# Linear attention and two MLPs in one program: the second product of the first MLP done two token blocks at a time, 512 columns a matmul

## The chip, the core and the metric

The kernel runs on one core of one Trainium2 chip. The metric is the device time of that core for one execution, in microseconds (us). TensorE (PE) multiplies, VectorE (DVE) and ScalarE (ACT) work element by element, GpSimd (POOL) does next to nothing here, and SyncE (SP) issues nearly all transfers (DMA) between device memory and the on-chip buffers.

## The reference

```python
kv  = einsum('bhsd,bhse->bhde', k, v)         # 8 batches, 8 heads, 576 steps, 64 wide
out = einsum('bhsd,bhde->bhse', q, kv)
x   = out / sqrt(mean(out*out) + 1e-6) * g_norm     # -> 4608 tokens x 512
h   = x @ moe_w_in                            # 512 -> 2048
x   = maximum(0.01*h, h) @ moe_w_out          # 2048 -> 512
h   = maximum(x @ moe2_w_in, 0)               # 512 -> 2048
out = (h*h) @ moe2_w_out                      # 2048 -> 512
```

All data is float32.

## The kernel before

The 4608 tokens are nine blocks (0 to 8) of 512. The program has four passes, each over all blocks: pass 1 is the attention and the first product with its leaky ReLU, pass 2 the second product of the first MLP, passes 3 and 4 the two products of the second MLP.

Every float32 operand is split into a high part (rounded to the format that TensorE reads at full rate, an ACT copy) and a low part (the rest, a DVE subtraction); a product is three matmuls: high by high, high by low, low by high. Passes 2 to 4 save further multiplications by a Strassen scheme in Winograd's form: both operands are cut into quarters (A11 to A22 for the weights, B11 to B22 for the activations in pass 2), sums of quarters are made (S1 to S4 from A, T1 to T4 from B), and seven products P1 to P7 of half size replace eight. `PRODUCTS` names their operands, `ORDER` the order in which they run, `SUMS` the sums. The weight sides of all seven are made in pass 1 and kept in device memory.

Pass 2 before goes block by block. A block's contraction of 2048 is cut in four groups n (`NQ`), and for each group `load_g2` loads two halves of the activations (`g_raw`), `sum_op` makes the four T sums on DVE, `hi_op` and `lo_op` make the seven operand pairs, and `second` issues 12 matmuls for each of the seven products: two chunks c, two output halves t, three split products. B's quarters split the block's 512 tokens in two halves of 256 (`U`), so every matmul of this pass moves 256 columns. The seven products add up in seven banks of the accumulation memory (PSUM) over the four groups. At a block's last group the banks are read and combined (`p1`, `u2`, `u3`, `u4` and the four outputs C11 to C22, by the `adder` on DVE or an ACT copy), and stored to `x2_d`.

Pass 3 (`first`) takes block 0 alone with 256 columns a matmul, then blocks 1 to 8 in pairs, where B's two column halves are the two blocks of a pair (`SETS`), with 512 columns. It is the same operand form as pass 2 has after the change: weights stationary, activations moving.

The order of all this is a table: each step gets a time in slots (`at_slot`), the steps are sorted by it and issued in that order, so it fixes the order of every engine's queue. `tick` counts the slots and issues the stores that have waited one, and `fetch` loads weights. On-chip data lives in `NBIG` = 46 buffers of 4 KB a partition, handed out in the order in which they came free; 28 of them hold the weights of pass 2 all through that pass.

Of the kernel before, what the change touches and what calls it, by code (L numbers as in the profile page):

```python
# [10 lines left out]
F32 = mybir.dt.float32  # L11
# [7 lines left out]
def tile_linear_attention_two_mlps(  # L19
# [26 lines left out]
    nc = tc.nc  # L46
# [106 lines left out]
    def give_big(*ns):  # L153
        big_free.extend(ns)
# [108 lines left out]
    def store(out, in_, *slots):  # L263
        stores.append([out, in_, slots, 0])
# [22 lines left out]
        w_s[w, n, name] = t  # L287

    w_staged = {}
    w_names = [[PRODUCTS[p][x] for p in ORDER] for x in range(2)]  # L290

    def store_w2(w, n, x):
        name = w_names[LEFT[w]][x]
        slot, half = divmod(NPR * n + x, 2)
        src = w_operand(w, n, name)
        if (w, slot) not in w_staged:
            w_staged[w, slot] = take_big([P, 2, 2, 2, P], F32R, f"wh{name}_{w[0]}{w[1]}_{n}")
        t, s = w_staged[w, slot]
        nc.scalar.activation(out=t[:, half, 0], in_=src, func=AF.Copy)
        nc.vector.tensor_tensor(  # L300
            out=t[:, half, 1], in0=src, in1=f32(t[:, half, 0]), op=ALU.subtract
        )
        if half:
            store(w3_d[w][slot], f32(t).rearrange("p b h c f -> p b (h c f)"), s)
        if x == NPR - 1:
            give_big(w_s.pop((w, n))[1])


    def w_pos(w, n, x):
        name = w_names[LEFT[w]][x]  # L310
        if name[0] in "ST":
            y = int(name[1]) - 1
        else:
            i, j = int(name[1]) - 1, int(name[2]) - 1
            k, o = (j, i) if LEFT[w] == 0 else (i, j)
            y = 4 + 2 * (1 - k) + o
        return NPR * (n % 2) + y

    def store_a(w, n):
        to = w2_d[w][n // 2]  # L320
        if w[1] == 0:
            for name in ("A11", "A12", "A22"):
                at0 = w_pos(w, n, w_names[0].index(name))
# [518 lines left out]
    def second(ph, gg, x, free):  # L842
        j, n = gg
        tick()
        pr = ORDER[x]
        if n == 0:
            bank[pr] = next_bank(f"ps{ph}_{j}_{pr}")
        ps = bank[pr]
        gname = PRODUCTS[pr][1 - ph]
        g = op_t[ph, gg, gname][0]  # L850
        last = n == NQ - 1
        for c in range(2):
            w = w2((ph, 1), 2 * n + c, x)
# [12 lines left out]
        drop_op(ph, gg, gname)
        if not last:
            return
        if pr == 1:
# [3 lines left out]
            u_t["u2"] = adder("gl", f"u2_{ph}{j}", bank[6], p1)  # L873
        elif pr == 7:
            u_t["u3"] = adder("stg", f"u3_{ph}{j}", ps, u_t["u2"])
        elif pr == 5:
            u_t["u4"] = adder("gh", f"u4_{ph}{j}", ps, u_t["u2"])
        outs = {2: ("C11", "p1"), 5: ("C22", "u3"), 4: ("C21", "u3"), 3: ("C12", "u4")}
        if pr in outs:
            name, x = outs[pr]  # L880
            e = adder("h", f"o{ph}{j}_{name}", ps, u_t[x])
            i, o = int(name[1]) - 1, int(name[2]) - 1
            if ph == 0:
                to = x2_d[j][2 * i:2 * i + 2].rearrange("c p t -> p c t")[:, :, o * U:(o + 1) * U]
# [33 lines left out]
    with tc.manual_schedule():  # L918
# [71 lines left out]
        def at_slot(t, *st):  # L990
            ev.append((t, st))

        def prep(z):
            n = (("os", 1), ("os", 2), ("oh", 2), ("oh", 11), ("ol", 2), ("oh", 0), ("ol", 11),
                 ("os", 3), ("ol", 0), ("oh", 3), ("oh", 1), ("ol", 3), ("ol", 1), ("os", 4))
            if z == "S":
# [4 lines left out]
            assert n[3] == ("oh", 11)  # L1001
            return [(kind, names.get(x) or f"{z}{x}") for kind, x in n]

        def second_pass(t0, ph, blocks):
            gs = [(j, n) for j in blocks for n in range(NQ)]
            steps = prep("TS"[ph])
            for x, gg in enumerate(gs):
                at0 = t0 + NPR * x
                ahead = 13 if ph and not x else 8
                at_slot(at0 - 18 if ahead > 8 else max(at0 - 14, t0 - 12), "gl", ph, gg)  # L1010
                for n, (kind, name) in enumerate(steps):
                    at_slot(
                        at0 - ahead + n * (ahead - 1) / len(steps) + 0.3, kind, ph, gg, name
                    )
# [101 lines left out]
        def drop_pairs(ps):  # L1116
# [84 lines left out]
```

## Time and profile before

| what | us |
|---|---|
| median of 3 runs (lowest, highest) | 1590.11 (1588.51, 1590.2) |
| the profiled execution | 1588.2 |
| its span, first to last instruction | 1586.4 |
| TensorE busy within the span | 1570.8 |
| VectorE busy | 1199.6 |
| ScalarE busy | 804.2 |

The span is what the trace covers; the profiled execution's own time is 1.8 us longer. Busy times count instructions at work, not waiting. Matmuls are pipelined, so one matmul's duration in the trace is longer than the distance from its start to the next one's start; rates are read from starts. Pass 1 lies from 0 to 504.6 us of the span, pass 2 to 867.5, pass 3 to about 1222.8 and pass 4 to the end.

### The profile page before, as it was taken

The numbers are of one execution on the slowest core, as the hardware profiler recorded it, in microseconds if no ns is written. First come the engines' busy times: TensorE is split into PE (matmuls) and PEld (weight loads), VectorE is DVE, ScalarE is ACT, GpSimd is POOL, SyncE is SP. The second block draws the span as 40 slices with busy tenths as digits, with TensorE's granted clock in tenths as the row PEclk, the third lists the DMA queues.
The fourth block names the chain that finished last, engine by engine and source line by source line (L and its number), as shares of the span: only waits on it lengthen the run. The fifth ranks groups of instructions, "written<-read, shape, count | busy, mean of one in ns | idle before, by whom it ended". The sixth has DMA issues, their size and how long they took to land. (4 is left out here: it accounts for less than half of the span.)

```text
span 1586.4 us, 27414 instructions
## 1 busy us (share of the span) xinstructions
PE 1570.8 (99%) x10604; PEld 1425.4 (90%) x10604; DVE 1199.6 (76%) x1952; ACT 804.2 (51%) x1429; POOL 7.2 (0%) x16
## 2 busy tenths in 40 slices
PE   8999999999999999999999999999999999999998
PEld 5788888888888999999999888888888999999998
DVE  6857777777765888777777877768777887777775
ACT  6856666666655444444444444535446544433442
POOL 0000000000000000000000000000000000000000
PEclk9999999999999999999999999999999999999999
DMA  9978899899579344433349444555569443333341
GB/s 255 284 220 284 257 308 294 292 282 348 190 244 296 107 141 145 128 129 127 124 128 335 140 163 162 185 169 186 165 214 356 161 142 128 124 129 127 126 126 72
DMA packets 239714, 309.04 MB, mean 195 GB/s; under 512 B 52192, under 2 KB 190944, under 8 KB 239584
## 3 DMA queue, kind: packets, MB, share of 16 engines
q1 hardware_dynamic: 238224, 306.74, 59.7%
q8 instruction: 83, 1.36, 0.4%
q10 hardware_dynamic: 1360, 0.56, 0.1%
q14 instruction: 47, 0.39, 0.1%
HBM read 183.50 MB, written 123.73 MB: 194 GB/s over the span
## 5 line engine op out<-in xcount | busy, mean ns | idle before, releaser
L666 PE MATMUL hps<-xh,w 128*128 128x512 f32 x1152 | 378.7, 396 | 2.1 <-ACT xh L623 1.3
L666 PEld LDWEIGHTS hps<-xh,w 128*128 128x128 f32 x1152 | 216.1, 188 | 49.8 <-DVE w L238 1.9
L666 PE MATMUL hps<-xl,w 128*128 128x512 f32 x576 | 224.6, 390 | 0.5 <-DVE xl L624 0.5
L666 PEld LDWEIGHTS hps<-xl,w 128*128 128x128 f32 x576 | 108.4, 188 | 22.6 <-issue 1.0
L678 ACT ACTIVATE h<-hps 128x512 f32<-128x512 f32 x144 | 84.9, 592 | 25.0 <-issue 10.2
L775 DVE TENSOR_TENSOR h_C<-aps,u 128x512 f32<-128x512 f32 x72 | 49.5, 688 | 35.4 <-PE aps L796 35.1
L775 DVE TENSOR_TENSOR u<-bps,p 128x512 f32<-128x512 f32 x72 | 49.5, 687 | 28.6 <-ACT p L806 19.0
L380 DVE TENSOR_TENSOR w<-w 128x512 fp32r<-128x512 f32 x56 | 37.8, 687 | 34.8 <-ACT w L379 30.6
L553 DVE TENSOR_TENSOR qhl<-qtps,qhl 128x512 fp32r<-128x512 f32 x32 | 22.1, 691 | 46.2 <-ACT qhl L552 46.2
L806 ACT ACTIVATE p<-aps 128x512 f32<-128x512 f32 x36 | 21.3, 592 | 69.9 <-PE aps L796 69.9
L796 PE MATMUL aps<-op_B21h,w 128*128 128x512 f32 (+1 forms) x160 | 52.0, 374 | 1.2 <-ACT p L806 1.2
L796 PE MATMUL bps<-op_T4h,w 128*128 128x512 f32 (+1 forms) x160 | 51.2, 369 | 0.6 <-DVE u L775 0.6
L205 DVE SCALAR_TENSOR_TENSOR w_raw<-w_raw 128x512 uint32<-128x512 uint32 x64 | 44.1, 688 | 9.8 <-ACT w_raw L204 9.3
L796 PE MATMUL aps<-op_B22h,w 128*128 128x512 f32 (+1 forms) x160 | 51.1, 368 | 0.0
L796 PE MATMUL bps<-op_T3h,w 128*128 128x512 f32 (+1 forms) x160 | 51.0, 368 | 0.0
L796 PE MATMUL bps<-op_T2h,w 128*128 128x512 f32 (+1 forms) x160 | 51.0, 368 | 0.0
L796 PE MATMUL aps<-op_B11h,w 128*128 128x512 f32 (+1 forms) x160 | 51.0, 368 | 0.0
L796 PE MATMUL aps<-op_T1h,w 128*128 128x512 f32 (+1 forms) x160 | 51.0, 368 | 0.0
L813 ACT ACTIVATE h_C<-aps 128x512 f32<-128x512 f32 x36 | 21.5, 599 | 57.5 <-issue 38.1
L775 DVE TENSOR_TENSOR u<-ps,p 128x512 f32<-128x512 f32 x18 | 12.4, 692 | 49.6 <-ACT p L871 49.6
L611 DVE TENSOR_TENSOR sqo<-sqo,y 128x512 f32<-128x512 f32 x32 | 22.1, 692 | 35.3 <-ACT y L609 35.3
L552 ACT ACTIVATE qhl<-qtps 128x512 fp32r<-128x512 f32 x32 | 19.1, 597 | 52.3 <-PE qtps L545 52.3
(1430 smaller groups left out, 4096.4 us busy)
## 6 DMA issues: line engine op xcount, KB each, us to landing
g_raw<-g SPq DMA_DIRECT2D x144, 512.0 KB, 5.4
g<-h SPq DMA_DIRECT2D x144, 256.0 KB, 5.0
g<-h_C SPq DMA_DIRECT2D x144, 256.0 KB, 2.5
w_raw<-in_moe_w_in_dram SPq DMA_DIRECT2D x32, 512.0 KB, 6.8
w_raw<-in_moe_w_out_dram SPq DMA_DIRECT2D x32, 512.0 KB, 7.0
x_raw<-x SPq DMA_DIRECT2D x32, 512.0 KB, 6.5
w<-w SPq DMA_DIRECT2D x56, 256.0 KB, 4.7
w<-w SPq DMA_DIRECT2D x28, 512.0 KB, 5.4
```

Of the source, the lines that this page charges most:

```text
L205: nc.vector.scalar_tensor_tensor(out=lower, in0=upper, scalar=0x80000000, in1=lower, op0=ALU.bitwise_and, op1=ALU.bitwise_or,)
L380: nc.vector.tensor_tensor(out=by_h[:, :, 1], in0=src[:, :, 1], in1=src[:, :, 0], op=ALU.subtract)
L552: nc.scalar.activation(out=t[:, 0], in_=ps, func=AF.Copy)
L553: nc.vector.tensor_tensor(out=t[:, 1], in0=ps, in1=f32(t[:, 0]), op=ALU.subtract)
L611: (nc.gpsimd if i == 1 else nc.vector).tensor_tensor(out=osb, in0=osb, in1=y, op=ALU.mult)
L666: nc.tensor.matmul(out=ps, lhsT=w[:, wh, c * P:(c + 1) * P], rhs=x_t[j][xh, c // 2][0][:, c % 2, :], start=(c == 0 and y == 0), stop=(c == ...
L678: nc.scalar.activation(out=h, in_=h_ps.pop((j, m)), func=AF.Prelu, alpha=0.01)
L775: nc.vector.tensor_tensor(out=t, in0=x, in1=y, op=ALU.add)
L796: nc.tensor.matmul(out=ps[:, p], lhsT=w[:, wh, c, :], rhs=t[xh][:, c, :], start=(fresh and p == 0 and c == 0 and y == 0), stop=(p == len(p ...
L806: nc.scalar.activation(out=p1, in_=ps, func=AF.Copy)
L813: nc.scalar.activation(out=h, in_=ps, func=AF.Relu)
```

## The change

Blocks 1 to 8 of pass 2 are taken in four pairs, as pass 3 takes them: the two column halves of B are the two blocks, so a matmul moves 512 columns. Within a pair the work goes product by product, each over all four groups n, in the new order `ORDER2` = 1, 6, 7, 2, 5, 4, 3. P2 is added onto P1's banks and P3 onto P5's, after P1 and P5 have been read. The T sums are made in place, over the quarter that is no longer wanted, in another but equivalent form (`D_SUMS`), and B22 is loaded a second time for T1 and P3. Pass 1 stores its result for these blocks in two tiles a group (`h_d`), so that each load is one contiguous tile of 128 x 1024. Block 0 keeps the old form with the new order. What comes below is the new core; line offsets and the smaller renamings are left out.

```diff
+    ORDER2 = (1, 6, 7, 2, 5, 4, 3)
 ...
 def leaky(j, m):
-        store(
-            g_d[0][j][m // 4][:, m % 2, :, (m // 2 % 2) * U:(m // 2 % 2 + 1) * U],
-            h.rearrange("p (t u) -> p t u", t=2),
-        )
+        if j:
+            store(h_d[j][m % 2][m // 4][:, m // 2 % 2], h)
 ...
+    PLACE = {"T3": "B12", "T2": "B11", "T4": "T3", "T1": "T2"}
+    D_SUMS = {
+        "T3": ("B22", "B12", ALU.subtract), "T2": ("T3", "B11", ALU.add),
+        "T4": ("B21", "T2", ALU.subtract), "T1": ("B22", "T2", ALU.subtract),
+    }
+    def pair_load(z, name, n):
+        t, slot = take_big([P, 2, TB], F32, f"d{name}_{z}_{n}")
+        k, o = int(name[1]) - 1, int(name[2]) - 1
+        nc.sync.dma_start(out=t, in_=h_d[SETS[z][o]][k][n])
+    def pair_sum(z, name, n):
+        x, y, op = D_SUMS[name]
+        to = d_t[z, PLACE[name], n]
+        nc.vector.tensor_tensor(out=to[0], in0=d_t[z, x, n][0], in1=d_t[z, y, n][0], op=op)
+    def pair_hi(z, x, n):
+        ts, slots = zip(*(take_big([P, 2, TB], F32R, f"dop{z}_{name}_{n}" + "hl"[y]) for y in range(2)))
+        nc.scalar.activation(out=ts[0], in_=d_t[z, name, n][0], func=AF.Copy)
+    def pair_lo(z, x, n):
+        nc.vector.tensor_tensor(out=lo, in0=d_t[z, name, n][0], in1=f32(hi), op=ALU.subtract)
+    def pair_second(z, x, n):
+        at = {2: 1, 3: 5}.get(pr, pr)
+        if n == 0 and at == pr:
+            bank["d", pr] = [next_bank(f"dps{z}_{pr}_{t}", 1)[:, 0] for t in range(2)]
+        ps = bank["d", at]
+        for c in range(2):
+            w = w2((0, 1), 2 * n + c, x)
+            for t in range(2):
+                for y, (wh, gh) in enumerate(((0, 0), (0, 1), (1, 0))):
+                    nc.tensor.matmul(out=ps[t], lhsT=w[:, wh, t, :], rhs=ops[gh][:, c, :], ...)
+        ...
+            if pr == 1:
+                nc.scalar.activation(out=u_t["p1", t], in_=ps[t], func=AF.Copy)
+            elif pr == 6:
+                u_t["u2", t] = adder("du2", f"du2_{z}{t}", ps[t], u_t["p1", t])
+            elif pr == 7:
+                u_t["u3", t] = adder("du3", f"du3_{z}{t}", ps[t], u_t["u2", t])
 ...
+        def pairs_pass(t0):
+            for z in range(1, len(SETS)):
+                def at_unit(w, *st):
+                    at_slot(t0 + 2 * w - 5.4, *st)
+                for n in range(NQ):
+                    loads = ((-10.4, "B12"), (-6.8, "B22"), (-2.8, "B11"), (2.2, "B21"), (12.2, "B22"))
+                    sums = ((-4, "T3"), (0, "T2"), (8, "T4"), (15, "T1"))
 ...
-        t2 = second_pass(t1, 0, list(range(NB)))
+        t2 = pairs_pass(second_pass(t1, 0, [0]))
```

On PE, at the point where pass 2 goes from block 0 to block 1, this stood before: six matmuls of 256 columns by one weight tile, then the next weight tile, and another product after 12 (`ps0_1_6` is the bank of block 1, product 6; `w2_01` is a weight tile).

```order
L860 MATMUL ps0_0_3_5534<-op0_(0, 3)_B22_5765,w2_01_27_5405 128x256 x6
L860 MATMUL ps0_1_6_5927<-op0_(1, 0)_T2_5789,w2_01_0_3783 128x256 x6
L860 MATMUL ps0_1_6_5927<-op0_(1, 0)_T2_5789,w2_01_3_4772 128x256 x6
L860 MATMUL ps0_1_1_5944<-op0_(1, 0)_B11_5803,w2_01_0_3783 128x256 x6
L860 MATMUL ps0_1_1_5944<-op0_(1, 0)_B11_5803,w2_01_4_5034 128x256 x6
```

Now, at the same point on PE, pair 1 starts with product 1; `dps1_1_0` and `dps1_1_1` are its two banks, `dop1_B11_0h` and `_0l` the high and low operand of group 0.

```order
L872 MATMUL ps0_0_3_5566<-op0_(0, 3)_B22_5814,w2_01_27_5437 128x256 x6
L953 MATMUL dps1_1_0_5957<-dop1_B11_0h_5862,w2_01_0_3815 128x512
L953 MATMUL dps1_1_0_5957<-dop1_B11_0l_5863,w2_01_0_3815 128x512
...
L953 MATMUL dps1_1_1_5958<-dop1_B11_0h_5862,w2_01_0_3815 128x512
L953 MATMUL dps1_1_1_5958<-dop1_B11_0l_5863,w2_01_0_3815 128x512
...
L953 MATMUL dps1_1_0_5957<-dop1_B11_0h_5862,w2_01_3_4804 128x512
L953 MATMUL dps1_1_0_5957<-dop1_B11_0l_5863,w2_01_3_4804 128x512
```

The 12 matmuls of a product and group are now one unit of 12 x 512 columns, and the next unit is the same product's next group.

On DVE the queue of a group before (block 2, group 2) has four sums (`sT1` to `sT4`) between seven low parts, all 512 elements long.

```order
L737 TENSOR_TENSOR sT1_0_(2, 2)_6537<-g_raw0_2_2_0_6415 128x512
L737 TENSOR_TENSOR sT2_0_(2, 2)_6539<-g_raw0_2_2_1_6417,sT1_0_(2, 2)_6537 128x512
L757 TENSOR_TENSOR op0_(2, 2)_T2_6545<-sT2_0_(2, 2)_6539,op0_(2, 2)_T2_6545 128x512
L757 TENSOR_TENSOR op0_(2, 2)_B11_6559<-g_raw0_2_2_0_6415,op0_(2, 2)_B11_6559 128x512
L737 TENSOR_TENSOR sT3_0_(2, 2)_6577<-g_raw0_2_2_1_6417,g_raw0_2_2_0_6415 128x512
L757 TENSOR_TENSOR op0_(2, 2)_B21_6574<-g_raw0_2_2_1_6417,op0_(2, 2)_B21_6574 128x512
```

Now the densest stretch of DVE's queue in a pair, around the end of product 6 of pair 1: low parts of T3 (`dop1_T3_..l`), the T4 sums written over T3 (`dB12_1_..`), and the two `du2` additions that read product 6's banks.

```order
L936 TENSOR_TENSOR dop1_T3_1l_6083<-dB12_1_1_5685,dop1_T3_1h_6082 128x1024
L921 TENSOR_TENSOR dB12_1_1_5685<-dB21_1_1_5976,dB11_1_1_5829 128x1024
L787 TENSOR_TENSOR du2_10_6099<-dps1_6_0_6035,dp1_10_6027 128x512
L787 TENSOR_TENSOR du2_11_6101<-dps1_6_1_6036,dp1_11_6029 128x512
L936 TENSOR_TENSOR dop1_T3_2l_6104<-dB12_1_2_5721,dop1_T3_2h_6103 128x1024
L921 TENSOR_TENSOR dB12_1_2_5721<-dB21_1_2_5995,dB11_1_2_5860 128x1024
L936 TENSOR_TENSOR dop1_T3_3l_6123<-dB12_1_3_5758,dop1_T3_3h_6122 128x1024
```

Sums and low parts have twice the length and half the number, and a sum for a later product stands between the low parts of the present one.

## Rows read from the trace of the kernel before

**Rows 1.** Page: span, PE's busy time, granted clock by slice (9: full)
```profile
span 1586.4 us, 27414 instructions
PE 1570.8 (99%) x10604; PEld 1425.4 (90%) x10604; DVE 1199.6 (76%) x1952; ACT 804.2 (51%) x1429; POOL 7.2 (0%) x16
PEclk9999999999999999999999999999999999999999
```

**Rows 2.** PE's waits: who for whom, us in total, times, longest
```profile
PE ssps L592 <- ACT sqo L576: 1.9, 3, 1.3
...
PE aps L796 <- ACT p L806: 1.2, 3, 0.7
```

**Rows 3.** Stretches: us, busy by engine (instructions), clock, DMA share, GB/s
```profile
0.00:504.60 504.60, 496.84 (x2877) 407.52 (x2878) 346.43 (x660) 323.56 (x618) 7.20 (x16) 1.00 0.86 272
...
544.90:867.50 322.60, 322.60 (x2691) 322.60 (x2690) 260.93 (x416) 132.22 (x233) 0.00 (x0) 1.00 0.48 157
867.50:1222.80 355.30, 352.31 (x1723) 296.68 (x1722) 273.97 (x373) 177.24 (x276) 0.00 (x0) 1.00 0.58 192
```

**Rows 4.** PE's timeline: first matmul of block 1, of pass 3 (start, length)
```profile
544.90 0.88 PE L860 MATMUL ps<-op_(1, 0)_T,w 128*128 128x256 f32 x6
...
867.46 0.28 PE L796 MATMUL bps<-op_T2h,w 128*128 128x256 f32 x1
```

**Rows 5.** Chain of waits, pass 3 with 512 columns (start, length, matmuls)
```profile
1109.23 2.72 PE aps L796 x12
1111.95 1.36 PE bps L796 x6
```

**Rows 6.** Matmuls and weight loads of block 1, group 0: shortest, median, longest ns
```profile
L860 PEld LDWEIGHTS ps<-op_(1, 0)_T,w x48: 192/192/192, 544.8 to 553.3; 128*128 128x128 f32 x48
L860 PE MATMUL ps<-op_(1, 0)_T,w x48: 283/283/283, 544.9 to 553.4; 128*128 128x256 f32 x48
```

**Rows 7.** Groups of DVE and ACT in pass 3, by shape: busy us, mean ns
```profile
L775 DVE TENSOR_TENSOR u<-bps,p 128x512 f32<-128x512 f32 x68 | 46.7, 687 | 26.3 <-ACT p L806 16.7 <-PE bps L796 9.6
L737 DVE TENSOR_TENSOR sT<-x_raw,sT 128x1024 f32<-128x1024 f32 x13 | 15.9, 1221 | 0.2
L757 DVE TENSOR_TENSOR op_T2l<-sT,op_T2h 128x1024 fp32r<-128x1024 f32 x7 | 8.6, 1226 | 4.3 <-ACT op_T2h L752 4.3
L806 ACT ACTIVATE p<-aps 128x512 f32<-128x512 f32 x34 | 20.1, 591 | 67.0 <-PE aps L796 67.0
L752 ACT ACTIVATE op_T4h<-sT 128x1024 fp32r<-128x1024 f32 x7 | 7.4, 1062 | 13.3 <-DVE sT L737 13.3
```

**Rows 8.** Transfers issued from 545 to 867 us: count, KB, us to landing
```profile
g_raw<-g SPq DMA_DIRECT2D x60, 512.0 KB, 5.4
x<-o_C SPq DMA_DIRECT2D x35, 256.0 KB, 4.9
...
x_raw<-x SPq DMA_DIRECT2D x6, 512.0 KB, 7.3
```

**Rows 9.** Timeline of DVE, ACT and PE at the start of pass 3
```profile
866.83 0.68 DVE L757 TENSOR_TENSOR op_T1l<-sT,op_T1h 128x512 fp32r<-128x512 f32 x1
867.42 0.68 DVE L737 TENSOR_TENSOR sT<-x_raw,sT 128x512 f32<-128x512 f32 x1
868.03 0.68 DVE L775 TENSOR_TENSOR o_C<-ps,u 128x512 f32<-128x512 f32 x1
868.22 0.63 ACT L752 ACTIVATE op_T4h<-sT 128x512 fp32r<-128x512 f32 x1 [6.13 <-DVE sT L737]
868.76 0.62 ACT L752 ACTIVATE op_B22h<-x_raw 128x512 fp32r<-128x512 f32 x1
870.53 0.60 ACT L806 ACTIVATE p<-aps 128x512 f32<-128x512 f32 x1 [1.16 <-PE aps L796]
871.18 0.38 PE L796 MATMUL aps<-op_B21h,w 128*128 128x256 f32 x1 [0.69 <-ACT p L806]
```

More of the change, by code (lines that the diff above doesn't have):

```diff
@@ L132, in tile_linear_attention_two_mlps @@
     g_d = [
-        [[dram.tile([P, 2, 2, TB], F32, name=f"g{ph}_{j}_{n}") for n in range(NQ)] for j in range(NB)]
+        [[dram.tile([P, 2, 2, TB], F32, name=f"g{ph}_{j}_{n}") for n in range(NQ)]
+         for j in range(NB if ph else 1)]
         for ph in range(2)
     ]
+    h_d = {
+        j: [[dram.tile([P, 2, TB], F32, name=f"h{k}_{j}_{n}") for n in range(NQ)] for k in range(2)]
+        for j in range(1, NB)
+    }
     big_free = list(range(NBIG))
@@ L289, in tile_linear_attention_two_mlps @@
     w_staged = {}
-    w_names = [[PRODUCTS[p][x] for p in ORDER] for x in range(2)]
+    w_names = {
+        w: [PRODUCTS[p][LEFT[w]] for p in (ORDER if w[0] else ORDER2)] for w in LEFT
+    }
     def store_w2(w, n, x):
-        name = w_names[LEFT[w]][x]
+        name = w_names[w][x]
         slot, half = divmod(NPR * n + x, 2)
@@ L309, in w_pos @@
     def w_pos(w, n, x):
-        name = w_names[LEFT[w]][x]
+        name = w_names[w][x]
         if name[0] in "ST":
@@ L678, in leaky @@
         nc.scalar.activation(out=h, in_=h_ps.pop((j, m)), func=AF.Prelu, alpha=0.01)
-        store(
-            g_d[0][j][m // 4][:, m % 2, :, (m // 2 % 2) * U:(m // 2 % 2 + 1) * U],
-            h.rearrange("p (t u) -> p t u", t=2),
-        )
+        if j:
+            store(h_d[j][m % 2][m // 4][:, m // 2 % 2], h)
+        else:
+            store(
+                g_d[0][j][m // 4][:, m % 2, :, (m // 2 % 2) * U:(m // 2 % 2 + 1) * U],
+                h.rearrange("p (t u) -> p t u", t=2),
+            )
         tick()
@@ L844, in second @@
         tick()
-        pr = ORDER[x]
+        pr = (ORDER if ph else ORDER2)[x]
         if n == 0:
@@ L872, in second @@
             u_t["p1"] = p1
-            u_t["u2"] = adder("gl", f"u2_{ph}{j}", bank[6], p1)
+        if pr == (1 if ph else 6):
+            u_t["u2"] = adder("gl", f"u2_{ph}{j}", bank[6], u_t["p1"])
         elif pr == 7:
@@ new lines, in pair_sum @@
+    def pair_sum(z, name, n):
+        x, y, op = D_SUMS[name]
+        to = d_t[z, PLACE[name], n]
+        nc.vector.tensor_tensor(out=to[0], in0=d_t[z, x, n][0], in1=d_t[z, y, n][0], op=op)
+        del d_t[z, PLACE[name], n]
+        d_t[z, name, n] = to
+        if name == "T3":
+            give_big(d_t.pop((z, "B22", n))[1])
+    def pair_hi(z, x, n):
+        name = PRODUCTS[ORDER2[x]][1]
+        ts, slots = zip(*(take_big([P, 2, TB], F32R, f"dop{z}_{name}_{n}" + "hl"[y]) for y in range(2)))
+        nc.scalar.activation(out=ts[0], in_=d_t[z, name, n][0], func=AF.Copy)
+        d_op[z, x, n] = ts, slots
@@ new lines, in pair_lo @@
+    def pair_lo(z, x, n):
+        name = PRODUCTS[ORDER2[x]][1]
+        hi, lo = d_op[z, x, n][0]
+        nc.vector.tensor_tensor(out=lo, in0=d_t[z, name, n][0], in1=f32(hi), op=ALU.subtract)
+        if name in ("B21", "T1", "T4", "B22"):
+            give_big(d_t.pop((z, name, n))[1])
+    def pair_second(z, x, n):
+        tick()
+        pr = ORDER2[x]
+        at = {2: 1, 3: 5}.get(pr, pr)
+        if n == 0 and at == pr:
+            bank["d", pr] = [next_bank(f"dps{z}_{pr}_{t}", 1)[:, 0] for t in range(2)]
+        ps = bank["d", at]
+        ops, slots = d_op.pop((z, x, n))
+        last = n == NQ - 1
+        for c in range(2):
+            w = w2((0, 1), 2 * n + c, x)
+            for t in range(2):
+                for y, (wh, gh) in enumerate(((0, 0), (0, 1), (1, 0))):
+                    nc.tensor.matmul(
+                        out=ps[t], lhsT=w[:, wh, t, :], rhs=ops[gh][:, c, :],
+                        start=(n == 0 and at == pr and c == 0 and y == 0),
+                        stop=(last and c == 1 and y == 2),
+                        skip_group_check=True,
+                    )
+        give_big(*slots)
+        if z == len(SETS) - 1:
+            d_done.update(NPR * (2 * n + c) + x for c in range(2))
+            for slot in range(NSLOT):
+                if ((0, 1), slot) in w_t and {2 * slot, 2 * slot + 1} <= d_done:
+                    drop_w(((0, 1), slot))
+        if not last:
+            return
+        for t in range(2):
+            if pr == 1:
+                u_t["p1", t] = take_mid("dp", [P, TB], f"dp1_{z}{t}")
+                nc.scalar.activation(out=u_t["p1", t], in_=ps[t], func=AF.Copy)
[3 more added lines that the diff above has]
+                u_t["u3", t] = adder("du3", f"du3_{z}{t}", ps[t], u_t["u2", t])
+            else:
+                name = {2: "C11", 5: "C22", 4: "C21", 3: "C12"}[pr]
+                if pr == 2:
+                    e = hp.tile([P, TB], F32, tag="h", name=f"do{z}_{name}{t}")
+                    nc.scalar.activation(out=e, in_=ps[t], func=AF.Copy)
+                else:
+                    e = adder("h", f"do{z}_{name}{t}", ps[t], u_t["u2" if pr == 3 else "u3", t])
+                i, o = int(name[1]) - 1, int(name[2]) - 1
+                store(x2_d[SETS[z][o]][2 * i + t], e)
@@ L991, in at_slot, with prep @@
             ev.append((t, st))
-        def prep(z):
+        def prep(z, first=False):
             n = (("os", 1), ("os", 2), ("oh", 2), ("oh", 11), ("ol", 2), ("oh", 0), ("ol", 11),
                  ("os", 3), ("ol", 0), ("oh", 3), ("oh", 1), ("ol", 3), ("ol", 1), ("os", 4))
-            if z == "S":
+            if first:
+                n = (("os", 1), ("oh", 11), ("ol", 11), ("os", 2), ("oh", 2), ("ol", 2), ("os", 3),
+                     ("oh", 3), ("oh", 0), ("ol", 3), ("oh", 1), ("ol", 0), ("ol", 1), ("os", 4),
+                     ("oh", 4), ("ol", 4), ("oh", 22), ("ol", 22))
+            elif z == "S":
                 n += (("oh", 22), ("oh", 4), ("ol", 22), ("ol", 4))
@@ L1005, in second_pass @@
             gs = [(j, n) for j in blocks for n in range(NQ)]
-            steps = prep("TS"[ph])
+            steps = prep("TS"[ph], not ph)
             for x, gg in enumerate(gs):
@@ L1017, in second_pass @@
                     at_slot(at0 + n + 0.1, "s2", ph, gg, n, True)
-                if gg[0] == blocks[-1]:
+                if ph and gg[0] == blocks[-1]:
                     at_slot(at0 + NPR, "wd", (ph, 1), gg[1])
@@ L1022, in tile_linear_attention_two_mlps @@
         at_slot(0, "lag", 5)
+        def pairs_pass(t0):
[5 more added lines that the diff above has]
+                    sums = ((-4, "T3"), (0, "T2"), (8, "T4"), (15, "T1"))
+                    if z == 1:
+                        loads = ((-6.2, "B12"), (-6.1, "B22"), (-2.2, "B11"), *loads[3:])
+                        sums = ((-3, "T3"), *sums[1:])
+                    for w, name in loads:
+                        at_unit(w + n, "pl", z, name, n)
+                    for w, name in sums:
+                        at_unit(w + n + 0.02, "pt", z, name, n)
+                    for x in range(NPR):
+                        at_unit(NQ * x + n, "ph", z, x, n)
+                        at_unit(NQ * x + n + 0.01, "po", z, x, n)
+                        at_slot(t0 + 2 * (NQ * x + n) + 0.1, "p2", z, x, n)
+                t0 += 2 * NPR * NQ
+            return t0
         t1 = 0
-        t2 = second_pass(t1, 0, list(range(NB)))
+        t2 = pairs_pass(second_pass(t1, 0, [0]))
         last = len(SETS) - 1
```

12 lines of the change are left out of this document (9 added, 3 removed).

## The prediction

> **What bounds the kernel now.** I read the page first: TensorE is busy for 1570.8 of the span's 1586.4 us, and its granted clock stands at full (the 2.4 GHz level) in all 40 slices [rows 1]. Then the list of PE's waits: the longest is 1.9 us in total, the one at pass 3's start 1.2 us in three times [rows 2]. Then the stretches: in blocks 1 to 8 of pass 2, from 544.90 to 867.50, PE is busy for 322.60 of 322.60 us, while DVE is busy for 260.93, ACT for 132.22, and the transfers take 0.48 of their engines at 157 GB/s [rows 3]. So the stretch that the change rewrites is nothing but a row of matmuls, without a gap; time can only go by making these matmuls take less of PE, and come back only as gaps.
>
> What a matmul takes of PE is the distance between starts. Block 1 starts at 544.90 and pass 3 at 867.46 [rows 4]; between them lie 8 blocks x 4 groups x 7 products x 12 = 2688 matmuls of 256 columns, so one takes 322.56 / 2688 = 120.0 ns. In pass 3, 12 matmuls of 512 columns take 2.72 us, 226.7 ns each [rows 5]. Twice 256 columns cost 240.0 ns as two matmuls and 226.7 as one: 13.3 ns are a price of the matmul, not of its columns.
>
> **The change, part by part.** *Fewer and wider matmuls.* The pairs do 4 x 7 x 4 x 12 = 1344 matmuls of 512 columns in place of the 2688: 1344 x 226.7 ns = 304.7 us against 322.6. That is 17.9 us less. The same instruction (weights stationary, 512 columns moving, three split products a weight pair) runs in pass 3 at this rate while DVE and ACT work on operands of the same form, so I take the rate as it is. The clock needs no term, since PE stays without gaps on both sides.
>
> *Supplying a unit.* A unit is the 12 matmuls of one product and group, 2.72 us. It needs a high part (ACT, 1024 elements, 1.06 us) and a low part (DVE, 1.23 us) [rows 7]. Per pair DVE has 28 low parts and 16 sums at 1.22 us and 10 additions at 0.69: 53.7 + 6.9 = 60.6 us of 28 x 2.72 = 76.2, a share of 0.80, against 260.93 / 322.60 = 0.81 before [rows 3, 7]. ACT has 28 x 1.06 + 4 x 0.6 = 32 us. Neither becomes the bound on average.
>
> What could still hurt is the order within a pair. In the built order the high part of most units waits for the matmuls of the unit three before it, whose buffers it takes; from that release there are two units, 5.44 us, until PE wants it. In the densest place, the end of product 6 in the order shown, DVE has two additions (1.4), then the low part, whose high part ACT makes meanwhile, then a sum (1.22) that the next low part stands behind. Release, high part 1.06, low part 1.23 is 2.3 us; with a sum and the two additions wholly in the way, 2.3 + 1.22 + 1.38 = 4.9. Both are under 5.44, so I cost the supply at 0. Without this cover each us beyond 5.44 costs a third of a us per unit, since a buffer comes round every third unit.
>
> *Loads.* A pair loads five tiles of 512 KB for each group instead of four: 20 x 0.524 + 8 outputs x 0.262 = 12.6 MB in 76.2 us, 165 GB/s, near the 157 that this stretch moves now and below the 192 of pass 3 [rows 3]. A 512 KB load of pass 2 lands after 5.4 us, the slowest kind there after 7.3 [rows 8]. Each load stands in SP's queue 2.8 units or more (7.6 us; in pair 1 at least 2.2, 6.0 us) ahead of the sum or copy that reads it. The tightest is the second B22: its buffer is free only after B21's low part, and T1's sum, behind which DVE's queue waits, comes next. 7.6 us and the two units of lead behind it cover 7.3. Cost 0; at a landing of 12 us, which no row shows, it would cost about the 2 us of rival 2 a pair.
>
> *Pass 1.* The same 256 KB stores, each now one run a partition in place of two. PE's gaps of pass 1 (504.60 - 496.84 = 7.8 us [rows 3]) are at the start and wait for engines, not for these stores: 0. Block 0 in the order 1, 6, 7 starts with a plain quarter, so its first operand needs no sum ahead: 0.
>
> *PSUM.* A pair opens ten banks; product 4 takes those of P1 and P2, whose last reader, an ACT copy of 0.6 us, has all of product 5 (10.9 us) to finish. P2 is added to P1 after products 6 and 7. No wait.
>
> *Pair 4 to pass 3.* Here a wait grows. Before, PE stands 0.69 us for the copy `p`, which ends at 871.13 [rows 9]. Ahead of it on ACT are two high parts that hang on DVE's T4 sum. Before, one output addition of DVE lay behind that sum. Now the last product ends with two additions, the second released by PE's very last matmul, and both stand ahead of T1's low part and the sum. From PE's end: 0.1 for the release, two steps of 0.6 and the sum's 0.68 on DVE, then 0.54 (the two copies' distance) and 0.62 on ACT; so `p` can start at 3.2 us, where PE would let it start at 2.9 (24 matmuls x 0.12). The wait becomes about 1.0 us: +0.3 us (0, if DVE gains on this, to +0.9, if another addition falls in between).
>
> *Passes 3 and 4* keep their instructions and, as the built order shows, their leads; the buffers only come round in another order: 0.
>
> Sum against the profiled execution: 1588.2 - 17.9 + 0.3 = 1570.6 us. The three timed runs lie at 1588.51 to 1590.2 with the median at 1590.11; their mean is 1.4 us above the profiled one. I carry that: **1572.0 us**. For the likeliest case alone I would say 1569.5 to 1575.
>
> **A rule that speaks against this.** The 13.3 ns come from [rows 4, 5]. The Trainium skill (TensorE: Matmul & The Clock Gate, section "Back-to-back issue gap") gives the isolated gap of a matmul as its columns at 2.4 GHz plus about 2.5 ns. By that rule the change would save only 1344 x 2.5 ns = 3.4 us, an estimate that would put the time at 1586.5, on rival 1's side. The trace does not agree: 120.0 and 226.7 ns lie 13.3 and 13.4 above their columns at 2.4 GHz [rows 4, 5].
>
> **The rivals.**
>
> 1. *The width is not what costs.* In pass 2 each weight load lasts 192 ns beside a matmul distance of 120 [rows 6]; perhaps something in this pass, as the loading of its weights, sets the pace by the column, and 512 columns stay at 2 x 120.0 = 240 ns. Then the change does not do what it says, and the time is 1588.2 + 0.3 + 1.4 = 1589.9, no change. Against it: pass 3 also loads 128 x 128 weights for every matmul, and keeps 226.7 at 512 columns. Chance 0.03.
>
> 2. *Short gaps where the pattern changes.* Block 0 to pair 1, four pair starts, and the second B22. At a pair's start the next B11, T3 and T2 fall together with the output additions, and B11's load is released only five units (13.6 us) before PE wants it: 7.3 landing + 1.06 + 1.23 + a sum and two additions in the way (2.6) is 12.2. If a landing runs 3.4 us longer than these rows have it, 2 us are lost per pair, 8 in all: 1580. Chance 0.09.
>
> 3. *Slower: the operand buffers come round too late.* Place: every unit of the four pairs, 112. The release of a unit's buffers, high part, low part and what DVE's queue puts ahead must fit into 5.44 us. The saving is 17.9 / 112 = 0.16 us per unit, and a chain of c costs (c - 5.44) / 3 per unit, so from c = 5.9 us on the kernel is slower. I get 2.3 to 4.9 [rows 7]. If a sum that waits for its load stands ahead each time, or DVE is held a further 1.6 us a unit, c is 6.5, the loss 0.35 x 112 = 40, and the time 1572 + 40 = 1612. For it: DVE's share of 0.80 leaves it little slack, and its queue is strictly in order. Against it: the price needs the worst order at every unit, while additions come at 5 of a pair's 28 units and sums at 16. Chance 0.05.
>
> **How the numbers follow.** The forecast 0.80, rival 1 0.03, rival 2 0.09, rival 3 0.05, the remaining 0.03 spread between 1580 and 1600. 0.2% (3.2 us) is about what a measurement of this kernel can tell from no change, so faster means below 1586.9. Faster: 0.80 + 0.09 + 0.01 of the remainder = 0.90; same: rival 1 and 0.01 = 0.04; slower: rival 3 and 0.01 = 0.06. The range reaches from 1568.5 (the profiled sum less the 0.3 and a run's scatter of 1.7) to 1580, where rival 2 ends; about 0.1 is left above it.
>
> **What will show it.** Right: PE's busy time falls by about 18 us; the first matmul of pass 3 starts about 18 us earlier; 12 wide matmuls of pass 2 take 2.72 us; PE's list of waits has nothing over 2 us from the pairs. The wait of pass 3's start for the copy `p` reads about 1.0 us. Rival 1 would show 12 in 2.88. Rival 2 would show PE waiting for `dop` tiles at the first unit of a pair, with a load behind it. Rival 3 would show a small wait at nearly every unit, behind low parts on DVE. The forecast is wrong if PE's idle time between 545 us and pass 3 is over 3 us, or if passes 3 and 4 change their length by more than 1.

## The result

The changed kernel takes 1576.09 us (median of runs from 1575.70 to 1578.01), the kernel before 1589.33 beside it: a ratio of 0.9918, 95% interval 0.9905 to 0.9930. That is 13.2 us faster. The forecast was 1572.0; the time lies in the range of 1568.5 to 1580, but above the likeliest case's own 1569.5 to 1575.

The profiled execution of the changed kernel took 1576.05 us. The page answers [rows 1]: 1344 matmuls fewer, PE busy for 13.5 us less, and the clock at 9 tenths or more in every slice of 39 us.

```profile
span 1574.3 us, 24420 instructions
PE 1557.3 (99%) x9260; PEld 1356.5 (86%) x9260; DVE 1173.9 (75%) x1760; ACT 798.3 (51%) x1325; POOL 7.2 (0%) x16
PEclk9999999999999999999999999999999999999999
```

The stretches answer [rows 3]. They are pass 1, block 0 of pass 2, the four pairs, pass 3 up to the wait at pass 4's start, and the rest. The columns are those of [rows 3].

```profile
0.00:505.27 505.27, 498.81 (x2876) 409.28 (x2877) 345.65 (x659) 323.80 (x618) 7.21 (x16) 0.99 0.85 271
505.27:547.20 41.93, 40.99 (x338) 40.48 (x337) 34.37 (x53) 21.27 (x37) 0.00 (x0) 1.00 0.70 239
547.20:856.13 308.93, 306.53 (x1346) 251.79 (x1345) 234.16 (x224) 126.66 (x131) 0.00 (x0) 1.00 0.54 180
856.13:1211.64 355.51, 352.27 (x1723) 296.70 (x1721) 274.79 (x374) 177.13 (x277) 0.00 (x0) 1.00 0.57 190
1211.64:1574.30 362.66, 358.76 (x2982) 358.30 (x2982) 284.98 (x454) 149.49 (x263) 0.00 (x0) 1.00 0.40 130
```

Each stretch begins at a first matmul of PE's timeline: block 0's, pair 1's, pass 3's [rows 4 has the last two of before]. That splits the 12.1 us between the two profiled spans exactly:

| stretch, us | before | after | difference | forecast |
|---|---|---|---|---|
| pass 1 | 504.58 | 505.27 | +0.69 | 0 |
| block 0 of pass 2 | 40.32 | 41.93 | +1.61 | 0 |
| blocks 1 to 8 of pass 2 | 322.56 | 308.93 | -13.63 | -17.9 |
| passes 3 and 4 | 718.94 | 718.17 | -0.77 | +0.3 |
| span | 1586.4 | 1574.3 | -12.1 | -17.6 |

So the wide matmuls did not bring back all that they take away. The list of PE's waits from 500 to 860 us says where PE stood (who for whom, us in total, times, longest); before it had none in pass 2.

```profile
PE dps L953 <- DVE dop_B_2l L936: 1.2, 1, 1.2
PE dps L953 <- DVE dop_B_1l L936: 1.0, 1, 1.0
PE ps L872 <- ACT op_(0, 1)_T L764: 0.6, 1, 0.6
PE ps L872 <- DVE op_(0, 1)_T L769: 0.3, 1, 0.3
```

PE's timeline shows both places (start, length, tile, count, idle before): T4 of block 0's group 1, then pair 1's units 0 to 4, marked by the first matmul of each high part (`dop_B_1h`: of group 1's B11) and, where PE waits, of the low part.

```profile
523.30 0.38 PE L872 MATMUL ps<-op_(0, 1)_T,w 128*128 128x256 f32 x1 [0.60 <-ACT op_(0, 1)_T L764]
524.03 1.57 PE L872 MATMUL ps<-op_(0, 1)_T,w 128*128 128x256 f32 x11 [0.34 <-DVE op_(0, 1)_T L769]
...
547.20 0.40 PE L953 MATMUL dps<-dop_B_0h,w 128*128 128x512 f32 x1
...
549.94 0.39 PE L953 MATMUL dps<-dop_B_1h,w 128*128 128x512 f32 x1
551.33 0.50 PE L953 MATMUL dps<-dop_B_1l,w 128*128 128x512 f32 x1 [1.00 <-DVE dop_B_1l L936]
...
553.96 0.39 PE L953 MATMUL dps<-dop_B_2h,w 128*128 128x512 f32 x1
555.52 0.50 PE L953 MATMUL dps<-dop_B_2l,w 128*128 128x512 f32 x1 [1.17 <-DVE dop_B_2l L936]
...
558.14 0.39 PE L953 MATMUL dps<-dop_B_3h,w 128*128 128x512 f32 x1
...
561.18 0.39 PE L953 MATMUL dps<-dop_T_0h,w 128*128 128x512 f32 x1
```

Units 1 to 3 take 4.02, 4.18 and 3.04 us where 12 matmuls at 226.7 ns take 2.72: 3.08 us over. Of the other 109 units 106 keep to 2.72; three, the last T1 unit of pairs 1 to 3, take 3.13, 3.09 and 3.13: 1.19 over. Together that is 4.27, and 308.93 - 4.27 = 304.66, the 1344 x 226.7 ns of the forecast. The width does what was said, and two small causes, with block 0, take a third of it back.

Of the T1 units the same view of three engines shows the chain: DVE's low part of group 2, DVE's sum of group 3, ACT's high part of group 3, DVE's low part, and PE, which comes to that low part 0.2 us early.

```profile
597.61 1.23 DVE L936 TENSOR_TENSOR dop_T_2l<-dB,dop_T_2h 128x1024 fp32r<-128x1024 f32 x1 [1.19 <-ACT dop_T_2h L930]
598.76 1.22 DVE L921 TENSOR_TENSOR dB<-dB,dB 128x1024 f32<-128x1024 f32 x1
600.07 1.06 ACT L930 ACTIVATE dop_T_3h<-dB 128x1024 fp32r<-128x1024 f32 x1 [2.49 <-DVE dB L921]
601.16 1.23 DVE L936 TENSOR_TENSOR dop_T_3l<-dB,dop_T_3h 128x1024 fp32r<-128x1024 f32 x1 [1.19 <-ACT dop_T_3h L930]
601.98 0.39 PE L953 MATMUL dps<-dop_T_3h,w 128*128 128x512 f32 x1
602.44 0.50 PE L953 MATMUL dps<-dop_T_3l,w 128*128 128x512 f32 x1
```

From low part to low part it is 601.16 - 597.61 = 3.55 us, where PE takes a unit in 2.72. Over four units the lead runs out.

### The profile page after: what moved, and what is told of

It reads as the page before. It is cut to its first block, busy times and chain, and to the rows that moved or that the text cites. A ratio compares the mean times of both kernels' runs of the same rounds, so it can differ in the third digit from the quotient of the medians.

```text
span 1574.3 us, 24420 instructions
## 1 busy us (share of the span) xinstructions
PE 1557.3 (99%) x9260; PEld 1356.5 (86%) x9260; DVE 1173.9 (75%) x1760; ACT 798.3 (51%) x1325; POOL 7.2 (0%) x16
## 5 line engine op out<-in xcount | busy, mean ns | idle before, releaser
L921 DVE TENSOR_TENSOR dB<-dB,dB 128x1024 f32<-128x1024 f32 x64 | 78.1, 1221 | 1.1
```

The source lines that it names most:

```text
L921: nc.vector.tensor_tensor(out=to[0], in0=d_t[z, x, n][0], in1=d_t[z, y, n][0], op=op)
```

## The experiments

My theory: a matmul's fixed price is what the change saves, 17.9 us, and 4.3 + 1.6 us come back because DVE is late, in block 0 through the new list of steps, behind it as a backlog, and at T1 through a serial chain. The rivals: the width saves less than that; the loads land late (rival 2 of the prediction); the supply is short at every unit (rival 3).

### Two matmuls of 256 columns in the place of one of 512

```diff
-    nc.tensor.matmul(out=ps[t], lhsT=w[:, wh, t, :], rhs=ops[gh][:, c, :], ...)
+    for s in range(2):
+        nc.tensor.matmul(out=ps[t][:, s * U:(s + 1) * U], lhsT=w[:, wh, t, :],
+                         rhs=ops[gh][:, c, s * U:(s + 1) * U], ...)
```

> The changed kernel with the width alone undone: each product of a pair of blocks is issued as two matmuls of 256 columns, one behind the other, with the same weights and operands; order of the products, sums in place and loads stay. Theory (the matmul's own price is what the change saves): 2688 matmuls at 120.0 ns in place of 1344 at 226.7 ns, so the pairs take 322.6 us and not 304.7, and the kernel 1576.1 + 17.9 = 1594.0 us; a unit is then 2.88 us long, so some of the waits of pair 1 and of the T1 products (4.3 us in all) may shrink, and 1591 to 1594 fits. Rival (the gain comes from the order, the sums in place or the transfers): 1576. Rival (a matmul costs its columns and a fixed 2.5 ns, the Trainium skill's TensorE page in Back-to-back issue gap): 1344 * 2.5 ns = 3.4 us more, 1579.5.

Measured: 1593.52 us, 1.0022 of the kernel before (1.0013 to 1.0031). The pairs' stretch, in the columns of the stretches above:

```profile
546.42:871.52 325.10, 323.17 (x2691) 322.70 (x2690) 235.86 (x224) 126.67 (x131) 0.00 (x0) 1.00 0.53 171
```

325.10 us, 16.2 more than with 512 columns. Units 1 to 3 still take 2.5 us over 2.88, and the T1 units no longer wait; without the 2.5 the stretch is 322.6, to the tenth what 2688 matmuls took before. So the order, the sums in place and the fifth load save nothing; the width alone saves all, and without it the change costs 3.6 us (1589.97 for the kernel before beside it). By the isolated gap of the Trainium skill (TensorE: Matmul & The Clock Gate, section "Back-to-back issue gap") the width would be worth 3.4 us here, an estimate; the trace has 17.9 without the waits.

### Pair 1's T2 sums behind the low parts that are wanted first

```diff
-    sums = ((-3, "T3"), *sums[1:])
+    sums = ((-3, "T3"), (2.5, "T2"), *sums[2:])
```

> In the first pair alone the four sums T2 are issued two and a half units later, behind the low parts of the first product (B11), which the first units need; loads stay. Theory (VectorE's queue is what makes units 1 to 3 of pair 1 late: it works without a gap from 537.5 to 560, and a T2 sum of 1.22 us stands ahead of each late low part): the 1.30 + 1.46 + 0.32 us that units 1 to 3 take over 2.72 go, 1576.1 - 2.7 to 3.1 = 1573.0 to 1573.4. Rival (the operands are late because their loads land late): no change, 1576.1. Rival (the sums become late for the T2 product's own units instead): the wait moves to units 4 to 7, 1575 to 1577.

Measured: 0.9901 of before (0.9886 to 0.9916), 1574.71 us. The pairs take 306.19 us in place of 308.93, block 0 stays at 41.93, and PE's waits for `dop_B_1l` and `dop_B_2l` are gone. The loads are the same, so they were not what came late: the queue of DVE was. The 2.7 us rest on this stretch: the intervals of the two ratios overlap, and the profiled execution itself is hardly shorter (1575.85 us against 1576.05), since pass 1, the same code in all these kernels, took 507.53 us in it and not 505.27.

### The T1 sums one unit earlier

```diff
-    sums = ((-4, "T3"), (0, "T2"), (8, "T4"), (15, "T1"))
+    sums = ((-4, "T3"), (0, "T2"), (8, "T4"), (14, "T1"))
```

> In every pair the four sums T1 are issued one unit earlier (14 units into the pair, not 15). Theory (the last T1 unit of pairs 1 to 3 starts 0.41 us late because sum, high part and low part of each unit run one behind the other, 1.22 + 1.06 + 1.23 us against a unit of 2.72): three times 0.41 go, 1574.9. Rival (the high part waits for the buffer that the low part before it gives back, and that keeps the loop as it is): 1576.1. Rival (the second load of B22 is then late for the sum, with 1.8 units or 4.9 us where 4.0 is the median of a load): the wait grows, 1577 to 1580.

Measured: 0.9910 of before (0.9896 to 0.9923), 1575.49 us. The pairs take 307.72 us, 1.21 less (this stretch shows it, the whole times' intervals overlap); no T1 unit is longer than 2.72, and no new wait stands in the list. DVE's low parts at T1 now follow one another at 2.35 us, since the sum is no longer between them:

```profile
595.43 1.23 DVE L936 TENSOR_TENSOR dop_T_2l<-dB,dop_T_2h 128x1024 fp32r<-128x1024 f32 x1 [1.16 <-ACT dop_T_2h L930]
597.78 1.23 DVE L936 TENSOR_TENSOR dop_T_3l<-dB,dop_T_3h 128x1024 fp32r<-128x1024 f32 x1 [1.13 <-ACT dop_T_3h L930]
```

### Another order of block 0's steps

```diff
-    n = (("os", 1), ("oh", 11), ("ol", 11), ("os", 2), ("oh", 2), ("ol", 2), ("os", 3),
-         ("oh", 3), ("oh", 0), ("ol", 3), ("oh", 1), ("ol", 0), ("ol", 1), ("os", 4),
-         ("oh", 4), ("ol", 4), ("oh", 22), ("ol", 22))
+    n = (("os", 1), ("oh", 11), ("os", 2), ("ol", 11), ("oh", 2), ("os", 3), ("oh", 3),
+         ("ol", 2), ("oh", 0), ("ol", 3), ("oh", 1), ("os", 4), ("ol", 0), ("oh", 4),
+         ("ol", 1), ("ol", 4), ("oh", 22), ("ol", 22))
```

> Block 0's steps alone are put in another order: each sum stands one step ahead of its high part and T4 two steps earlier; the order of its products stays. Theory (block 0 lasts 41.93 us instead of 40.32 since the list of steps makes VectorE wait for ScalarE three times in group 1 and T4's high part comes 0.60 us late): the 1.6 us go from block 0; since VectorE is full behind it, up to 1.6 us may come back as longer waits in units 1 to 3 of pair 1, so 1574.5 to 1576.1, and block 0 itself at 40.3 to 40.6 us. Rival (the five low parts of weights that VectorE does in a row at 518.8 make T4 late, whatever the list): block 0 stays at 41.9.

Measured: 0.9886 of before (0.9872 to 0.9899), 1571.88 us: 4.2 under the changed kernel, more than the 1.6 I had put on it. Block 0 takes 40.31 us, and the pairs 305.84, together 4.7 less: the waits of pair 1 went too. First DVE's timeline of the changed kernel in block 0's group 1, and the first low part of pair 1 that came late:

```profile
511.92 0.68 DVE L749 TENSOR_TENSOR sT_(0, 1)_5463<-g_raw,sT_(0, 1)_5427 128x512 f32<-128x512 f32 x1
513.30 0.69 DVE L769 TENSOR_TENSOR op_(0, 1)_T<-sT_(0, 1)_5463,op_(0, 1)_T 128x512 fp32r<-128x512 f32 x1 [0.70 <-ACT op_(0, 1)_T L764]
513.91 0.68 DVE L749 TENSOR_TENSOR sT_(0, 1)_5481<-g_raw,g_raw 128x512 f32<-128x512 f32 x1
515.82 0.69 DVE L389 TENSOR_TENSOR w<-w 128x512 fp32r<-128x512 f32 x1 [1.22 <-ACT w L388]
...
518.83 3.09 DVE L389 TENSOR_TENSOR w<-w 128x512 fp32r<-128x512 f32 x5
521.84 0.68 DVE L749 TENSOR_TENSOR sT_(0, 1)_5545<-g_raw,sT_(0, 1)_5463 128x512 f32<-128x512 f32 x1
523.28 0.69 DVE L769 TENSOR_TENSOR op_(0, 1)_T<-sT_(0, 1)_5545,op_(0, 1)_T 128x512 fp32r<-128x512 f32 x1 [0.76 <-ACT op_(0, 1)_T L764]
...
550.07 1.21 DVE L936 TENSOR_TENSOR dop_B_1l<-dB,dop_B_1h 128x1024 fp32r<-128x1024 f32 x1
```

And the same places in the experiment:

```profile
513.69 0.69 DVE L749 TENSOR_TENSOR sT_(0, 1)_5520<-g_raw,sT_(0, 1)_5448 128x512 f32<-128x512 f32 x1
...
514.90 3.09 DVE L389 TENSOR_TENSOR w<-w 128x512 fp32r<-128x512 f32 x5
...
518.51 0.68 DVE L769 TENSOR_TENSOR op_(0, 1)_T<-sT_(0, 1)_5520,op_(0, 1)_T 128x512 fp32r<-128x512 f32 x1
...
543.72 1.22 DVE L936 TENSOR_TENSOR dop_B_1l<-dB,dop_B_1h 128x1024 fp32r<-128x1024 f32 x1
```

In the changed kernel a sum is followed at once by its own high part (ACT) and low part (DVE), so DVE stands 0.7 to 1.2 us each time until ACT is done (the 1.22 is for a weight's high part, which stands behind T3's in ACT's queue). T4's low part comes at 523.28, behind five low parts of weights that stand even ahead of its sum; PE wanted T4 at 522.5. With each sum a step ahead of its high part, T4's sum is done before the five, and its low part comes at 518.51. The five stand there in both, so they alone were not the cause. The kernel before has them there too, and a wait of 0.76 us for T4's high part:

```profile
516.00 3.10 DVE L380 TENSOR_TENSOR w<-w 128x512 fp32r<-128x512 f32 x5
519.01 0.69 DVE L737 TENSOR_TENSOR sT_(0, 1)_5513<-g_raw,sT_(0, 1)_5397 128x512 f32<-128x512 f32 x1
520.45 0.69 DVE L757 TENSOR_TENSOR op_(0, 1)_T<-sT_(0, 1)_5513,op_(0, 1)_T 128x512 fp32r<-128x512 f32 x1 [0.76 <-ACT op_(0, 1)_T L752]
```

There T4's low part comes 15.87 us after block 0's first matmul, in time; in the changed kernel it comes 18.01 us after it, and what is new are the waits of 0.70 and 1.22 ahead of it. The experiment shortens these waits and moves T4 ahead of the five at once, so it does not show whether one of the two would have been enough.

DVE is then 6.35 us earlier at `dop_B_1l` (6.1 counted from block 0's first matmul), and the additions and sums that stand ahead of pair 1's low parts are done in time. The backlog of pair 1 was made in block 0.

### Both edits

Block 0's steps as in the last experiment, and the T1 sums one unit earlier.

> Both edits together in the changed kernel: block 0's steps in the new order and the T1 sums one unit earlier. Theory (two separate causes, VectorE waiting for ScalarE in block 0's steps, and a serial sum, high part and low part at T1): block 0 at 40.3 us, the pairs at 1344 * 226.7 ns = 304.7 us, nothing waits between the first matmul of block 0 and pass 3; 1571.9 - 1.2 = 1570.7 us. Rival (the T1 sums, moved up, come into the stretch in which VectorE is full and delay an operand elsewhere): 1571.9 or more, with a new wait in the pairs.

Measured: 0.9886 of before (0.9869 to 0.9902), 1571.23 us, 4.9 under the changed kernel. Block 0 and the pairs:

```profile
505.59:545.90 40.31, 40.31 (x337) 40.31 (x336) 37.63 (x56) 22.43 (x38) 0.00 (x0) 1.00 0.74 254
545.90:850.57 304.67, 304.67 (x1347) 252.34 (x1345) 230.91 (x219) 125.41 (x129) 0.00 (x0) 1.00 0.56 181
```

PE is without a gap from block 0 to pass 3, at 304.67 us for the pairs. This is the best version. That it beats the last experiment rests on the stretch (304.67 against 305.84), not on the whole times, whose intervals overlap.

### Half of each low part worked out twice

On the last kernel, as a probe of how much room the supply has:

```diff
     nc.vector.tensor_tensor(out=lo, in0=d_t[z, name, n][0], in1=f32(hi), op=ALU.subtract)
+    nc.vector.tensor_tensor(out=lo[:, 0], in0=d_t[z, name, n][0][:, 0], in1=f32(hi[:, 0]),
+                            op=ALU.subtract)
```

> As the kernel with both edits, but VectorE works out the first half of each low part of the pairs twice (112 additions of 512 elements on top; the values stay). It is a probe of the rival by which operands become late in every unit. A pair's units need 57.95 us of VectorE in 76.2, or 2.07 us a unit of 2.72; with 0.60 us more it is 2.67. Theory (the supply is bound by VectorE's rate, and the lead of two units carries the rest): nearly hidden, 0 to 4 us, 1571 to 1575. Rival (the serial step from high part to low part and the waits for a buffer leave no room, so each addition shows): 112 * 0.60 = 67 us, 1638.

Measured: 1602.58 us, 1.0082 of before (1.0067 to 1.0097). Neither expectation holds: of the 67 us of added work 30.8 show (the pairs take 335.43), where I expected 0 to 4. DVE is busy for 304.87 us, as long as the pairs take without a wait (304.67) and longer than the 112 x 2.67 = 299 that I had reckoned, so a stretch in which it falls behind can't be made up. Two things make the low parts late. The first is that DVE is full in places. Where a sum for a later product stands between two low parts, it goes from low part to low part without a gap and still needs 711.37 - 708.37 = 3.00 us, where PE needs 2.72:

```profile
708.37 1.22 DVE L936 TENSOR_TENSOR dop_B_2l<-dB,dop_B_2h 128x1024 fp32r<-128x1024 f32 x1
709.62 0.69 DVE L937 TENSOR_TENSOR dop_B_2l<-dB,dop_B_2h 128x512 fp32r<-128x512 f32 x1
710.23 1.22 DVE L921 TENSOR_TENSOR dB<-dB,dB 128x1024 f32<-128x1024 f32 x1
711.37 1.22 DVE L936 TENSOR_TENSOR dop_B_3l<-dB,dop_B_3h 128x1024 fp32r<-128x1024 f32 x1
```

The second is a chain, at T4, where no sum stands between:

```profile
697.86 1.22 DVE L936 TENSOR_TENSOR dop_T_3l<-dB,dop_T_3h 128x1024 fp32r<-128x1024 f32 x1 [1.19 <-ACT dop_T_3h L930]
699.11 0.69 DVE L937 TENSOR_TENSOR dop_T_3l<-dB,dop_T_3h 128x512 fp32r<-128x512 f32 x1
```

```profile
696.76 1.06 ACT L930 ACTIVATE dop_T_3h<-dB 128x1024 fp32r<-128x1024 f32 x1 [2.08 <-DVE dop_T_2l L937]
699.89 1.06 ACT L930 ACTIVATE dop_B_0h<-dB 128x1024 fp32r<-128x1024 f32 x1 [2.06 <-DVE dop_T_3l L937]
```

The high part of a unit waits for the low part of the unit before it, whose source buffer it takes over, and the low part waits for its high part: one chain, 699.89 - 696.76 = 3.13 us a unit. Counted over the trace, 60 units take longer than 2.72 us: 43 of them come behind a DVE that worked without a gap and hold 23 of the 30.8 us, 15 come behind the chain and hold 6.2. The theory failed because it took the average of a pair: a lead of two units does not carry four and more units in a row that each need 3.0 us and more.

Without the added work the chain runs at 2.35 us (597.78 - 595.43 above), and a stretch with a sum would take about 3.00 - 0.60 = 2.40, an estimate from these rows (the changed kernel has 2.39 from 557.24 us on). So the room per unit is 0.3 to 0.4 us there, not the 0.65 that DVE's share leaves. This is the shortage of rival 3, a small wait at many units, though the chain is another than the one it named (a source buffer given back by the low part before, not an operand's by the matmuls three units before); the changed kernel stays under this point in all but the units named above.

### Four matmuls of 128 columns

The edit of the first experiment with four quarters, on the kernel with both edits.

> As the kernel with both edits, but each product of the pairs is issued as four matmuls of 128 columns, 5376 in place of 1344. Theory (a matmul costs its columns and a fixed 13.3 ns, as 120.0 ns for 256 columns and 226.7 ns for 512 give): 53.3 + 13.3 = 66.7 ns each, the pairs 358.4 us, the kernel 1570.7 + 53.7 = 1624 us. Rival (behind the narrow matmuls the weight load is the bound: the engine that loads weights is busy 5.00 of 5.00 us at 256 columns, some 113 ns a load): 5376 * 107 to 120 ns = 575 to 645 us, 1841 to 1911. Rival (a fixed 2.5 ns, the Trainium skill's TensorE page in Back-to-back issue gap): 4032 * 2.5 ns = 10 us more, 1581.

Measured: one run, 1865.97 us, within what the first rival gives. A stretch of its pairs:

```profile
600.00:1100.00 500.00, 500.00 (x4480) 500.00 (x4479) 195.76 (x178) 108.63 (x111) 0.00 (x0) 1.00 0.30 95
```

500 / 4480 = 111.6 ns a matmul, in place of the 66.7 that columns and 13.3 ns would give. Every matmul brings its own weight load (PEld), 4479 for 4480, even where the weights are those of the one before. The Trainium skill (TensorE: Matmul & The Clock Gate, section "LDWEIGHTS (loading the stationary operand)") gives a load of 128 columns as 128 / 1.2 = 106.7 ns; the trace has 5 ns more. So "columns and a fixed 13.3 ns" fits the two widths that gave it, 256 and 512, and fails at 128. That the load is what holds the matmuls at 111.6 ns is likely and not shown: PEld is busy for all of the time at 256 columns too [rows 3], and no run takes the load away from its matmul. What makes up the 13.3 ns stays open.

## Why the prediction was right, and where not

The mechanism was right, and its main term to 0.1 us: the two 256-column halves bring back 17.9 us, and the pairs without waits last 304.67. The rates of pass 3 and of pass 2 before held. The rest, step by step:

- *Block 0 "in the order 1, 6, 7 starts with a plain quarter, so its first operand needs no sum ahead: 0"*. This step failed. I looked at the first operand alone, not at the list of 18 steps that came with the order. It made T4 late in group 1 (nearly all of the +1.61 us) and DVE some 6 us late by the end of the block, which gave the 3.1 us of pair 1: 4.7 in all. The other order of the steps removed both.
- *Supplying a unit, 0.* Wrong by 1.2 us at T1. I had counted what stands ahead after a buffer's release and compared it once with 5.44 us; there a chain of 3.55 us repeats for four units, and the lead is used up by the fourth. That the sum of this product stands in the chain itself, and not only in its way, was not in my count.
- *Loads, 0; PSUM, 0.* Right: no wait of PE in the pairs has a transfer or a bank behind it, and later sums with the same loads removed the waits of pair 1.
- *Pair 4 to pass 3, +0.3, the wait "about 1.0".* Here 0.9 in place of 0.69 [rows 9]. Right. The row is PE's longest wait on `p`:

```profile
PE aps L808 <- ACT p L818: 1.3, 3, 0.9
```

- *Passes 3 and 4, 0.* Up to pass 4's wait +0.1 (355.51 against 355.39). The 0.9 us less after it lie behind the last matmul: 4.8 us to the span's end before, 3.9 after. It comes back in the profiles of all the variants (718.15 to 718.28 behind pass 3's start), but with one trace of before I can't say why.
- *Pass 1, 0.* 0.7 more in this profile; in those of the variants pass 1 ends between 504.48 and 507.53, and 504.48 is reached by the same code, so this is scatter; it goes with a load's landing (last section).
- *The 1.4 us carried from the profiled execution to the median.* They hold for the kernel before, whose runs beside the later kernels have medians of 1589.12 to 1589.97: its profiled 1588.2 was a fast execution. The changed kernel's was an ordinary one, 1576.05 against a median of 1576.09, so there was nothing to carry.

Profiled against profiled, the forecast was 1570.6 and the run 1576.05: +1.6 block 0, +4.3 pairs, +0.7 pass 1, -1.1 passes 3 and 4. Rival 2 named the places, block 0 to pair 1 and the second B22, from which T1 is made, but another cause, a late load. So it is luck in part that the time lies in the range: the room above the likeliest case was left for late loads, and two terms put at 0 used it. PE's gaps between 545 us and pass 3 came to 2.4 us (308.93 - 306.53), under the 3 at which I had called the forecast wrong. The matmuls of the trace overlap, so a short wait shows only in part as a gap; counted by starts, the waits cost 4.3.

## What to carry to other kernels

When a change brings its own list of steps for the engines ahead of the critical one, read the whole list in their order: a sum, its high part and its low part in direct succession on two in-order engines make both wait, and the debt is paid where the next stage begins. Check a supply by the period of its slowest serial chain against the consumer's period, not by busy share and one lead: 3.55 us against 2.72 fails after four units, at a share of 0.76 for the pairs. Check the share by stretches too, and not over a pair: in the probe of the low parts, units in a row that each needed 3.0 us were late although I had reckoned a mean of 2.67. Widening a matmul pays as much as its per-matmul price times the count, and only the rows at both widths tell that price; the price between 256 and 512 columns did not hold at 128.

## What the hardware showed that I had not expected

- A narrow matmul does not get cheap. With a 128 x 128 load of its own, each matmul of 128 columns took 111.6 ns in the pairs, also where the weights stay the same; at 256 columns, the kernel before, it was only 8.4 ns more. The transposes of pass 1, 128 columns with a load each, start 108 to 110 ns apart (one lasts 0.27 us, a row of four 0.60), so 111.6 is not the least that such a matmul takes:

```profile
19.16 0.60 PE L554 MATMUL qtps<-ident,q_raw 128*128 128x128 f32 x4
```

- The start of pass 1 scatters. PE's wait for `v_raw` at 6 us and the length of pass 1 go roughly together over the nine profiles, whose code is the same up to there: 0.4 and 504.58 us (before), 0.5 and 504.48, 0.8 and 505.00, 1.0 and 505.39, 1.1 and 505.12, 1.4 and 505.27 (the changed kernel), 1.2 and 505.59, 1.4 and 505.57, 1.8 and 507.53. That is up to 3 us which no edit made, as much as the smaller edits moved. The waits differ by 1.4 us only, so the load's landing alone is not shown to be the cause.
- The granted clock fell in two of these nine starts. In the changed kernel's profile it read 0.78 and 0.54, about the 1.2 GHz level, from 20 to 30 us, and the fall began in a stretch in which PE was busy for 2.93 of 5.00 us:

```profile
20.00:25.00 5.00, 2.93 (x4) 0.59 (x4) 4.56 (x9) 4.29 (x9) 0.00 (x0) 0.78 1.08 260
25.00:30.00 5.00, 4.98 (x15) 3.76 (x16) 4.30 (x8) 3.49 (x7) 0.00 (x0) 0.54 1.11 211
```

In the profile with the T2 sums later it read 0.95 and 0.71 from 5 to 15 us, behind the wait of 1.8, and pass 1 was the longest there. But from 20 to 25 us PE was busy for only 2.33 us in another profile (both edits), and the clock read 1.00. Pass 1 was no longer in the changed kernel's profile than in one without a fall (505.27 against 505.57). What lets the clock fall there stays open.
